# Plain tiles in place of two Strassen quads for one head group, another order of one group's band sets, and later queue clocks in the plan

## The chip, the cores and the metric

The kernel runs on one core of a Trainium2 chip. The metric is the time on the device in microseconds (us). The kernel before takes 650.26 us, the median of 3 runs from 650.11 to 650.94. Its profile shows one execution, with a span of 648.3 us from the first to the last instruction.

## The reference

Two branches work on the same `x` of 2048 tokens by 1024 and are mixed by a gate. Branch A is attention with 32 heads of 32 channels, in which each token looks at 8 tokens at a distance of 2. Branch B is a gated MLP with a product along the sequence.

```python
def _A_ref(x, wqkv, wo):
    H, Dh, W, dil = 32, 32, 8, 2
    q, k, v = ...                                  # x @ wqkv, by heads
    idx = pos[:, None] - (jnp.arange(W) * dil)[None, :]
    logits = einsum('bhsd,bhswd->bhsw', q, k[idx]) * Dh ** -0.5   # masked where idx < 0
    attn = softmax(logits)
    return einsum('bhsw,bhswd->bhsd', attn, v[idx]) @ wo

def _B_ref(x, w_in, w_sp, b_sp, w_out):
    z = gelu(x @ w_in)
    z1, z2 = z[..., :Fh], layernorm(z[..., Fh:])   # Fh = 1792
    g = einsum('ts,bsf->btf', w_sp, z2) + b_sp
    return (z1 * g) @ w_out

g = sigmoid((x * gate_w).sum(-1, keepdims=True))
out = g * A + (1 - g) * B
```

## The kernel before

The heads are worked on in 8 groups of 4 heads (128 channels). For each group TensorE makes q and k, transposed, then the band: for every block of 64 tokens the products with the 71 keys that it can see. ScalarE copies the band out of PSUM, it goes to DRAM and comes back in a skewed layout (`att_L`), and VectorE does the softmax and the products with v. All this is interleaved with the large products of both branches on TensorE. A plan made at build time, with a clock for each engine and for the transfer queue (`SP`, `DMA`), decides where in each engine's order the attention operations and transfers are put.

There are two ways to make q and k of a group. The plain way has 8 tiles of 8 matmuls, each 512 columns:

```python
def qk_tile(g, t, c, bank=low_bank):               # t: q or k, c: 512 tokens
    ps = bank()
    for kt in range(KT):                           # KT = 8
        nc.tensor.matmul(ps[:], w[:, t, kt, :], xT[:, kt, 512 * c:512 * (c + 1)], ...)
    act(0.5, pe(T_QK) + 0.2)
    nc.scalar.copy(dst[:, :, 256 * c:256 * (c + 1)], ps[:]...)
```

The Strassen way (Winograd's form) has two quads. A quad makes two blocks of q and two of k with 7 products of 4 matmuls in place of 8 products; it needs sums of the weights (`qk_sums`) and of `x` (`x_sums`, in `xts`), and copies and adds between the PSUM banks:

```python
def chain(...):                                    # used by qk_quad and z2_quad; generator
    X, Y, Z, V = bank_roles[side]                  # four banks: 0 to 3 or 4 to 7
    product(X, pairs(A11, B11), True, N);  nc.scalar.copy(Y[:, n], X[:, n]);  yield    # seed
    product(V, pairs(S1, T1), True, N);    share(vs, V[:, n]);                yield
    product(Y, pairs(S2, T2), False, N);   plus(Z, Y);                        yield    # VectorE add
    product(X, pairs(A12, B21), False, N); put(0, 0, X);                      yield
    product(Y, pairs(S3, T3), False, N);   plus(V, Y); put(1, 1, V);          yield
    product(Z, pairs(S4, B22), False, N);  put(0, 1, Z);                      yield
    product(W, pairs(A22, T4), False, N);  put(1, 0, W);                      yield
```

Two small matmuls (`mark`) go ahead of a quad on banks in which its later products are to add to what another engine wrote. Groups 2 to 5 are Strassen quads in both kernels. In the kernel before group 1 is too: its quads run one after the other, alone, and start just before the gate's transpose:

```python
    def x_sums(c): ...                             # 4 sums of 2048 elements for half c
    for c in range(4):                             # start: q, k of group 0, v of groups 0 to 2, bands of group 0
        ...
        if c > 1:
            x_sums(c - 2)
        if c == 2:
            load_wqk(2, sync.dma_start)
        ...
    for f in qk_sums(1):
        f()
    first_quad = qk_quad(1, 0, 0)
    for _ in range(2):
        next(first_quad)
    gate_mm = nc.tensor.matmul(glT, gl_s[:], ident32[:], start=True, stop=True)
    ...                                            # tanh, two VectorE operations, two stores
    settle(); live[0] = True                       # from here the plan is in force
    band_data[0], band_free[0], v_data[0] = T_START        # (0.0, 0.0, 0.0)
    clock["SP"], clock["DMA"] = 0.5, 1.5
    next_bands(); ...                              # att_L of group 0, g_att, v of group 0
    dma(0.0, 3.7, load_wvr, lambda t: fill.extend(... sums4_steps(wvs, ...)))   # weights of v_quad and their sums
    load_wqk_later(3, 0.0)

    def play_group(g):
        if g == 0:
            run(first_quad, step=step)
            run(qk_quad(1, 1, 0), step=step)
        elif g + 1 in PAIRS: ...                   # PAIRS = (2, 4)
```

The v of groups 0 to 2 is stored to DRAM by GpSimd's queue while the kernel starts:

```python
            (nc.gpsimd if i < 16 else sync).dma_start(dv, st[:, :, g * C:(g + 1) * C])
```

The band of a group is made in three sets, 0 with 2 blocks (16 matmuls) and 1 and 2 with 7 (56 matmuls). All use banks 4 to 7, so ScalarE must have copied one set out before the next is made. Group 7 has no next group to prepare; its sets stand among four plain tiles of z2 (8 matmuls of 448 columns each), after which the quads of z2 follow in pairs, one on each side:

```python
    BAND_SETS = [(0, 8, 2), (1, 1, 7), (9, 1, 7)]
    def group_tiles(g):                            # last line: g = 7
        ...
        return [tiles[0], band[1], tiles[1], band[0], tiles[2], band[2], tiles[3]]
    ...
        def quad_step():
            if n == 0 and count[0] == 0:
                mark(bank_roles[1][1:3], ZC)
            step(); ...
        run(*[z2_quad(*q) for q in quads[n:n + 2]], step=quad_step)
```

Of the kernel before, what the change touches and what calls it, by code (L numbers as in the profile page):

```python
# [13 lines left out]
P = 128  # L14
S = 2048
D = 1024
# [4 lines left out]
NG = NH // HG  # L21
# [37 lines left out]
def kernel(  # L59
# [238 lines left out]
    def vp_tile(i, bank=None, middle=None):  # L298
        ps = bank() if bank else banks[i % 2]
        for kt in range(KT):  # L300
            if kt == (2 if i else 6) and middle is not None:
                middle()
            nc.tensor.matmul(ps[:, 0:VP + 1], xT[:, kt, i * P:(i + 1) * P], wvp[:, kt, :], start=(kt == 0), stop=(kt == KT - 1))  # L303
        st = vp_slots[i // 4]
        nc.scalar.copy(st[:, i % 4, :].rearrange("p (g d h) -> p g d h", g=GP, h=HG), ps[:, 0:VP].rearrange("p (g h d) -> p g d h", g=GP, h=HG))
        nc.scalar.copy(gl_s[:, i:i + 1], ps[:, VP:VP + 1])
        if i % 4 == 3:
            for g in range(GP):
                dv = bass.AP(tensor=v_d.tensor, offset=v_d.offset + (g * (S + 16) + 16 + (i - 3) * P) * C, ap=[[C, P], [P * C, 4], [1, C]])
                (nc.gpsimd if i < 16 else sync).dma_start(dv, st[:, :, g * C:(g + 1) * C])  # L310

# [68 lines left out]
    def first_bands(c):  # L380
        band_blocks(0, *((0, 8, 2), (1, 1, 6, 3), (4, 1, 4, 2), (6, 1, 4, 2))[c])

    def x_sums(c):
        for r in range(4):
            lo, hi = slice(512 * c, 512 * c + 512), slice(1024 + 512 * c, 1536 + 512 * c)
            a, b = ((xT[:, 0:4, hi], xT[:, 0:4, lo]), (xT[:, 4:8, hi], xts[0][:, :, lo]),
                    (xT[:, 4:8, hi], xT[:, 0:4, hi]), (xT[:, 4:8, lo], xts[1][:, :, lo]))[r]
            nc.vector.tensor_tensor(xts[r][:, :, lo], a, b, ALU.subtract)  # L388

    quad = [0]  # L390
# [75 lines left out]
    def chain(A11, A12, A22, S1, S2, S3, S4, B11, B21, B22, T1, T2, T3, T4, vs, put, share, N, flip=False, side=None, lean=False, done=None):  # L466
# [8 lines left out]

        if side is None:
            side = quad[0] % 2
            quad[0] += 1
        X, Y, Z, V = bank_roles[side]
        bank_roles[side] = [X, V, Y, Z] if lean else [Y, V, X, Z]  # L480
        n = slice(0, N)
        dur, copy = N / 600.0 + 0.01, N / 1400.0 + 0.22
# [345 lines left out]
    LEAN = (True, True)  # L828
    T_START = (0.0, 0.0, 0.0)

    def square(n, x, junk):
# [6 lines left out]
        return nc.scalar.activation(junk, src, ACT.Square, accum_out=(s2, s2h)[x][:, n:n + 1])  # L838

    NQ = (0, 0, 0, 0, 0, 0, 0, 0)  # L840
    quads = [(0, i) for i in range(7)] + [(1, i) for i in range(8)]
# [3 lines left out]
    qv_slots = [reg(R_OFF + 34752 + 1024 * r, 1024).bitcast(F32) for r in range(2)]  # L845
    q_landed, q_free = {}, [1, 1]

# [47 lines left out]
    def play_group(g):  # L895
        if g == 0:
            run(first_quad, step=step)
            run(qk_quad(1, 1, 0), step=step)
        elif g + 1 in PAIRS:
            among_bands(g, qk_quad(g + 1, 0, 0))  # L900
            first = qk_quad(g + 1, 1, 0)
            for _ in range(2):
                next(first)
                step()
            mark(bank_roles[1][1:3], 512)
            run(qk_quad(g + 2, 0, 1), first, step=step)
        elif g in PAIRS:
            among_bands(g, qk_quad(g + 1, 1, 0))
        else:
            return False  # L910
        return True

    def group_tiles(g):
        if g + 1 < NG:
            tiles = [lambda t=t, c=c: qk_tile(g + 1, t, c) for t in range(2) for c in range(4)]
        else:
            tiles = [lambda a=a, m=m: z2_tile(7, a, m) for m in range(2) for a in range(2)]
        if g == 0:
            return tiles

        def band(x):
            band_set(g, x)
            if x == 2:
                bands_have[0] = g + 1
        band = [lambda x=x, f=band: f(x) for x in range(3)]
        if g - 1 in PAIRS and g + 1 < NG:
            return tiles[0:2] + [tiles[2], band[0], tiles[3], band[1], tiles[4], tiles[5], band[2]] + tiles[6:]
        if g + 1 < NG:
            return [tiles[0], band[0], tiles[1], band[1], tiles[2], tiles[3], band[2]] + tiles[4:]
        return [tiles[0], band[1], tiles[1], band[0], tiles[2], band[2], tiles[3]]  # L930

# [37 lines left out]

    for c in range(4):  # L970
        tiles = range(4 * c, 4 * c + 4) if c else ()
        for n, i in enumerate(tiles if c < 3 else ()):
            vp_tile(i, low_bank)
            if n == 0:
                first_bands(c - 1)
        if c > 1:
            x_sums(c - 2)
        if c == 2:
            load_wqk(2, sync.dma_start)
        for t in range(2):  # L980
            qk_tile(0, t, c, (lambda: banks[1 + t]) if c == 3 else low_bank)
            if c == 3 and t == 0:
                first_bands(2)
    for i in tiles:
        vp_tile(i, lambda: banks[3 * (i % 2)])
        if i == 12:
            first_bands(3)
    for f in qk_sums(1):
        f()

    first_quad = qk_quad(1, 0, 0)
    for _ in range(2):
        next(first_quad)
    glT = banks[7][0:16, 0:P]
    gate_mm = nc.tensor.matmul(glT, gl_s[:], ident32[:], start=True, stop=True)
    gate_act = nc.scalar.activation(omg[:], glT, ACT.Tanh, scale=0.5)
    nc.vector.tensor_scalar(g_s[:], omg[:], 0.5, 0.5, ALU.mult, ALU.add)
    gate_vec = nc.vector.tensor_scalar(omg_h[:], omg[:], -0.5, 0.5, ALU.mult, ALU.add)
    sync.dma_start(bass.AP(tensor=g_d.tensor, offset=g_d.offset, ap=[[P, 16], [1, P]]), g_s[:])
    gate_dma = sync.dma_start(bass.AP(tensor=og_d.tensor, offset=og_d.offset, ap=[[P, 16], [1, P]]), omg_h[:])  # L1000

    settle()
# [5 lines left out]
    band_data[0], band_free[0], v_data[0] = T_START  # L1008
    clock["SP"], clock["DMA"] = 0.5, 1.5
    stored.clear()  # L1010
# [3 lines left out]
    next_v(1)  # L1014
    def load_wvr():
        for m in range(2):
            sync.dma_start(wvr[m], wq_v[:, :, 2 * D + VP + VH * m:2 * D + VP + VH * (m + 1)])

    dma(0.0, 3.7, load_wvr, lambda t: fill.extend((t + LATE, 0.75, f) for f in sums4_steps(wvs, wvr[0][:, 0:4], wvr[0][:, 4:8], wvr[1][:, 0:4], wvr[1][:, 4:8])))
    load_wqk_later(3, 0.0)  # L1020
    next_v()
    q_free[:] = [1, 1]
    if 2 in PAIRS:
# [27 lines left out]
    for n in range(0, len(quads), 2):  # L1051
# [10 lines left out]
        def quad_step():  # L1062
            hold[0] = count[0] != 1
            if n == 0 and count[0] == 0:
                mark(bank_roles[1][1:3], ZC)
            step()
            count[0] += 1
            if p == 1 and i < 7 and count[0] in SQ_AT and squares[0][0] < 2 * i and len(squares) > 32 - SQH:
                act(0.9, clock["PE"])
                square(*squares.pop(0), None)  # L1070
        run(*[z2_quad(*q) for q in quads[n:n + 2]], step=quad_step)
    hold[0] = False
# [587 lines left out]
```

## Time and profile before

| what | value |
|---|---|
| time, median of 3 runs | 650.26 us |
| span in the profile | 648.3 us |
| TensorE matmuls | 637.5 us busy, 4345 recorded |
| VectorE | 519.3 us busy |
| ScalarE | 298.1 us busy |
| granted TensorE clock | 1.000 |
| groups 1 to 7 with their bands | about 42 to 181 us |
| z2, z1 and the rest of attention | about 182 to 345 us |

In the rows of slices each digit is the busy tenth of 1/40 of the span, here 16.2 us. In the timelines a row is a run of instructions of one kind: start, duration from the first to the last, engine, line of the kernel, operation, output and input, and their number; in square brackets is the idle time ahead of it and what ended it. PE is TensorE, DVE is VectorE, ACT is ScalarE, and SPq is the queue in which SyncE issues transfers. A few per cent of the matmul records are missing, so a count may be one or two short of the code's.

### The profile page before, as it was taken

Reading aid. Unit: us, or ns where it says so; the run is one execution under the profiler, and the core shown is the slowest. Engines: PE = TensorE matmul, PEld = TensorE weight load, DVE = VectorE, ACT = ScalarE, POOL = GpSimd, SP = SyncE. Lnnn points to the kernel's source line nnn. Section 1 sums busy time; section 2 is a strip of 40 time slices with the busy share of each in tenths; the row PEclk is TensorE's granted clock in tenths of the full one; section 3 lists DMA queues with packets and bytes.
Section 4 is the critical chain, followed back from the end, with each engine's and each line's share of the span. In section 5 each row is a group of like instructions: output and inputs, shape, how many; then the busy total and the mean of one; then the engine's idle time right before and its main releaser. Section 6 shows DMA issues by size and latency. Waiting matters only on the chain.

```text
span 648.3 us, 11298 instructions
## 1 busy us (share of the span) xinstructions
PE 637.5 (98%) x4345; PEld 336.2 (52%) x4391; DVE 519.3 (80%) x816; ACT 298.1 (46%) x644; POOL 15.4 (2%) x27
## 2 busy tenths in 40 slices
PE   8999999999999999999999999999999999999997
PEld 4544467444455555444444444444444444868684
DVE  0347998999899999999988766987569999586852
ACT  3547677676786878799643121121121121202120
POOL 2210000000000000001000000000000000000000
PEclk9999999999999999999999999999999999999999
DMA  9979564798687012258994578369487383557501
GB/s 218 202 162 283 115 153 103 175 226 197 133 216 201 1 51 76 66 160 233 259 257 130 130 166 189 100 202 283 91 190 174 84 158 102 107 138 127 124 28 49
DMA packets 227174, 98.19 MB, mean 151 GB/s; under 512 B 174496, under 2 KB 214064, under 8 KB 227120
## 3 DMA queue, kind: packets, MB, share of 16 engines
q1 hardware_dynamic: 226256, 95.70, 61.2%
q0 software_dynamic: 576, 1.57, 0.9%
q8 instruction: 34, 0.56, 0.4%
q10 hardware_dynamic: 288, 0.20, 0.1%
q14 instruction: 20, 0.16, 0.1%
HBM read 44.31 MB, written 36.61 MB: 125 GB/s over the span
## 4 chain that ended last, share of the span: by engine, by line
PE 90%; ACT 4%; SPq 2%; DMA 1%; DVE 1%; issue 1%; DVEq 0%; ACTq 0%
PE psum_all L402 71%; PE psum_all L1484 8%; PE psum_all L293 6%; PE psum_all L303 2%; PE psum_all L355 2%; ACT arena L838 2%; ACT arena L1175 1%; PE psum_all L790 1%; SPq L178 1%; DMA arena<-in_A_wqkv_dram 1%; SPq L194 1%; ACT arena L363 1%; ACT arena L783 1%; DMA arena<-zg_d 1%; DVE psum_all L473 0%
## 5 line engine op out<-in xcount | busy, mean ns | idle before, releaser
L402 PE MATMUL psum_all<-arena 128*128 128x512 f16 (+6 forms) x2481 | 502.5, 362 | 3.3 <-issue 0.8
L402 PEld LDWEIGHTS <-arena 128*128 128x128 f16 (+1 forms) x2518 | 244.9, 98 | 253.4 <-issue 3.2
L676 DVE TENSOR_TENSOR arena<-arena,att_A 128x2048 f16<-128x2048 bf16 x64 | 75.5, 1220 | 0.3
L473 DVE TENSOR_TENSOR psum_all<-psum_all,arena 128x512 f32<-128x512 f32 (+1 forms) x78 | 51.0, 669 | 8.7 <-PE psum_all L402 5.7
L1484 PE MATMUL psum_all<-arena 128*128 128x256 f16 (+1 forms) x468 | 51.6, 273 | 0.0
L1484 PEld LDWEIGHTS <-arena 128*128 128x128 f16 x468 | 45.8, 98 | 5.5
L293 PE MATMUL psum_all<-arena 128*128 128x512 bf16 x183 | 42.0, 379 | 1.2 <-issue 0.8
L420 ACT COPY psum_all<-psum_all 128x512 f32<-128x512 f32 (+1 forms) x24 | 12.5, 519 | 66.2 <-PE psum_all L402 65.5
L783 ACT ACTIVATE arena<-psum_all 128x448 bf16<-128x448 f32 x64 | 34.2, 545 | 18.3 <-PE psum_all L402 9.0
L1175 ACT ACTIVATE arena<-psum_all 128x512 bf16<-128x512 f32 x56 | 31.4, 613 | 19.8 <-PE psum_all L402 9.0
L680 DVE TENSOR_TENSOR arena<-arena 128x2048 f16<-128x2048 f16 x32 | 37.9, 1218 | 0.0
L363 ACT CAST arena<-psum_all 128x1988 f16<-128x1988 f32 (+3 forms) x25 | 33.9, 1358 | 2.7 <-PE psum_all L355 2.3
L838 ACT ACTIVATE arena<-arena 128x896 bf16<-128x896 bf16 x32 | 30.9, 981 | 0.0
L545 DVE TENSOR_TENSOR arena<-arena 128x512 f16<-128x512 bf16 (+5 forms) x60 | 30.1, 534 | 0.4
L444 ACT COPY psum_all<-psum_all 128x512 f32<-128x512 f32 (+1 forms) x24 | 12.3, 518 | 37.5 <-PE psum_all L402 36.8
L293 PEld LDWEIGHTS <-arena 128*128 128x128 bf16 x192 | 18.1, 98 | 21.5 <-DMA arena<-in_A_wqkv_dram 0.6
L869 ACT CAST arena<-psum_all 128x512 bf16<-128x512 f32 x40 | 22.2, 592 | 12.4 <-DVE psum_all L473 9.8
L388 DVE TENSOR_TENSOR arena<-arena 128x2048 f16<-128x2048 bf16 x8 | 9.4, 1221 | 20.9 <-DMA arena<-in_A_x_dram 20.7
L486 ACT COPY psum_all<-psum_all 128x512 f32<-128x512 f32 (+1 forms) x39 | 21.7, 570 | 6.6 <-PE psum_all L402 6.0
L426 ACT COPY arena<-psum_all 128x512 f32<-128x512 f32 (+1 forms) x24 | 12.7, 533 | 26.1 <-PE psum_all L402 22.5
L431 ACT COPY psum_all<-psum_all 128x512 f32<-128x512 f32 (+1 forms) x24 | 12.4, 517 | 25.8 <-PE psum_all L402 24.8
L549 DVE TENSOR_TENSOR arena<-arena 128x1024 f16<-128x1024 f16 (+1 forms) x16 | 11.4, 715 | 15.7 <-PE psum_all L402 15.7
(113 smaller groups left out, 530.3 us busy)
## 6 DMA issues: line engine op xcount, KB each, us to landing
arena<-v_d SPq DMA_DIRECT2D x8, 960.0 KB, 5.8
z_d<-arena SPq DMA_DIRECT2D x14, 512.0 KB, 3.9
arena<-z_d SPq DMA_DIRECT2D x14, 512.0 KB, 4.4
zg_d<-arena SPq DMA_DIRECT2D x56, 128.0 KB, 2.2
arena<-zg_d SPq DMA_DIRECT2D x32, 224.0 KB, 3.2
band_d<-arena SPq DMA_DIRECT2D x28, 248.5 KB, 4.2
arena<-in_A_wqkv_dram SPq DMA_DIRECT2D x16, 256.0 KB, 4.2
o_d<-arena SPq DMA_DIRECT2D x4, 1024.0 KB, 5.7
```

What stands on the lines that cost most here:

```text
L293: nc.tensor.matmul(ps[:], w[:, t, kt, :], xT[:, kt, 512 * c:512 * (c + 1)], start=(kt == 0), stop=(kt == KT - 1))
L363: nc.scalar.copy(dst, src)
L402: nc.tensor.matmul(bank[:, 0:N], lhsT, rhs, start=(start and m == 0), stop=(m == n - 1), skip_group_check=True)
L473: last_add[0] = nc.vector.tensor_tensor(out[:, n], a[:, n], vs, ALU.add)
L545: return [lambda a=a: nc.vector.tensor_tensor(*a) for a in args]
L676: lambda ws=ws, in0=in0, in1=in1: tt(p5[:, ws], in0[:, ws], in1[:, ws], ALU.mult)), False
L680: lambda a=p3[:, ws], b=p3[:, ws.start + 4:ws.stop + 4]: tt(a, a, b, ALU.add)), not n
L783: nc.scalar.activation(z2[:, i + 8 * a, ZC * c:ZC * (c + 1)], bank[:, 0:ZC], ACT.Gelu_apprx_tanh, accum_out=s1[:, 4 * n + c:4 * n + c + 1])
L838: return nc.scalar.activation(junk, src, ACT.Square, accum_out=(s2, s2h)[x][:, n:n + 1])
L869: nc.scalar.copy((qT_slots, kT_slots)[t][g % 2][:, :, 256 * (c + 2 * x):256 * (c + 2 * x + 1)], bank[:].rearrange("p (n e) -> p e n", e=2))
L1175: last_gelu[0] = nc.scalar.activation(z1s[:, f, a, :], bank[:], ACT.Gelu_apprx_tanh)
L1484: nc.tensor.matmul(bank[:, h], l, r, start=(start and m == 0), stop=(m == len(ab) - 1), skip_group_check=True)
```

## The change

Group 1 is made of plain tiles: one before the gate, seven after it. The sums of `x` are written after the gate. The stores of v go through SyncE's queue, the weights of the v quads are loaded and summed in the start, and the plan's clocks for SyncE and the transfers begin 8 us and 7 us later, so that the plan fits a queue that is still at work on these. In group 7 the small band set moves from between two tiles into the first quad of z2, after that quad's first product; the quad on the other side starts after its second. The rest follows from these: the counter of quads counts all quads, and `q_free` starts with one slot free. The purpose is fewer sums and adds on VectorE around the start of attention, a plan nearer to what the queue does, and no small band set that waits on ScalarE.

```diff
-                (nc.gpsimd if i < 16 else sync).dma_start(dv, st[:, :, g * C:(g + 1) * C])
+                sync.dma_start(dv, st[:, :, g * C:(g + 1) * C])
...
+        if c == 1:
+            for m in range(2):
+                sync.dma_start(wvr[m], wq_v[:, :, 2 * D + VP + VH * m:2 * D + VP + VH * (m + 1)])
...
+    qk_tile(1, 0, 0)
+    (gate, as before)
+    def x_sums(r):
+        for c in range(2): ...
+    for r in range(4):
+        x_sums(r)
...
-    T_START = (0.0, 0.0, 0.0)
+    T_START = (0.5, 0.0, 2.5)
...
+    sums4(wvs, wvr[0][:, 0:4], wvr[0][:, 4:8], wvr[1][:, 0:4], wvr[1][:, 4:8])
...
-        if g == 0:
-            run(first_quad, step=step)
-            run(qk_quad(1, 1, 0), step=step)
-        elif g + 1 in PAIRS:
+        if g + 1 in PAIRS:
...
-            tiles = [lambda t=t, c=c: qk_tile(g + 1, t, c) for t in range(2) for c in range(4)]
+            tiles = [lambda t=t, c=c: qk_tile(g + 1, t, c) for t in range(2) for c in range(4)][not g:]
...
-        return [tiles[0], band[1], tiles[1], band[0], tiles[2], band[2], tiles[3]]
+        return [tiles[0], band[1], tiles[1], tiles[2], band[2], tiles[3]]
...
-    for f in qk_sums(1):
-        f()
-
-    first_quad = qk_quad(1, 0, 0)
-    for _ in range(2):
-        next(first_quad)
...
-    clock["SP"], clock["DMA"] = 0.5, 1.5
+    clock["SP"], clock["DMA"] = 8.5, 8.5
...
-    def load_wvr(): ...
-    dma(0.0, 3.7, load_wvr, lambda t: fill.extend((t + LATE, 0.75, f) for f in sums4_steps(wvs, ...)))
     load_wqk_later(3, 0.0)
...
-            if n == 0 and count[0] == 0:
-                mark(bank_roles[1][1:3], ZC)
...
-        run(*[z2_quad(*q) for q in quads[n:n + 2]], step=quad_step)
+        two = [z2_quad(*q) for q in quads[n:n + 2]]
+        if n == 0:
+            for m in range(2):
+                next(two[0])
+                step()
+                if m == 0:
+                    band_set(NG - 1, 0)
+                    bands_have[0] = NG
+                    step()
+            mark(bank_roles[1][1:3], ZC)
+            two = two[::-1]
+        run(*two, step=quad_step)
```

## The prediction

> **What bounds the kernel now.** I read the page's busy shares first, then the slices, then the chain that ended last, and only then the stretch in which the change acts.
>
> ```profile
> span 648.3 us, 11298 instructions
> ...
> PE 637.5 (98%) x4345; PEld 336.2 (52%) x4391; DVE 519.3 (80%) x816; ACT 298.1 (46%) x644; POOL 15.4 (2%) x27
> ...
> PE   8999999999999999999999999999999999999997
> ...
> DVE  0347998999899999999988766987569999586852
> ...
> PEclk9999999999999999999999999999999999999999
> ...
> PE 90%; ACT 4%; SPq 2%; DMA 1%; DVE 1%; issue 1%; DVEq 0%; ACTq 0%
> ```
>
> TensorE is busy in every slice, at full granted clock, and carries 90% of the chain. VectorE is nearly full from about 55 to 300 us, but it does not hold TensorE up: the list of TensorE's waits over the whole run adds to some 5 us, with no entry after VectorE but two at the start. So time changes by what is added to or taken from TensorE's queue, and by small waits. These are the places the change touches (columns: start, duration, engine, line, operation, count):
>
> ```profile
> 42.63 1.89 PE L402 MATMUL psum_all<-arena 128*128 128x512 bf16 x7
> 44.45 0.39 PE L995 MATMUL psum_all<-ident,gl_s 128*16 128x128 f32 x2
> 44.78 11.83 PE L402 MATMUL psum_all<-arena 128*128 128x512 f16 x51
> 56.53 0.27 PE L355 MATMUL psum_all<-arena 32*64 32x64 bf16 x16
> ...
> 143.17 5.34 PE L293 MATMUL psum_all<-arena 128*128 128x512 bf16 x23
> 148.44 0.27 PE L355 MATMUL psum_all<-arena 32*64 32x64 bf16 x16
> ...
> 175.75 0.65 PE L355 MATMUL psum_all<-arena 32*64 32x71 bf16 x56
> 176.34 1.69 PE L790 MATMUL psum_all<-arena 128*128 128x448 bf16 x8
> 178.64 0.27 PE L355 MATMUL psum_all<-arena 32*64 32x64 bf16 x16 [0.61 <-ACT arena L363]
> ```
>
> Three plain q/k tiles, 24 matmuls (one record is missing), take 148.44 − 143.17 = 5.27 us; about 0.1 us of it is the change-over to the band matmuls. That gives 0.2155 us a matmul, without stalls. The Strassen run from 44.78 to 56.53 is 52 matmuls by the code: 20 left of the first quad, 28 of the second, 4 of the next group's. It takes 11.75 us where 52 × 0.2155 = 11.21, so 0.54 us is lost, 0.1 of it at the change-over. The lost 0.44 us is what a quad that runs alone pays for its adds and copies. The last lines show one real wait: in group 7 the small band set stands 0.61 us because ScalarE still empties the set before it.
>
> The queue that issues the transfers, and the first work that waits for them:
>
> ```profile
> 34.78 8.40 SPq L189 DMA_DIRECT2D band_d<-arena  x12
> 45.90 0.35 SPq L189 DMA_DIRECT2D g_d<-g_s  x1
> 46.35 0.37 SPq L189 DMA_DIRECT2D og_d<-omg_h  x1
> 46.82 1.29 SPq L189 DMA_DIRECT2D att_L<-band_d  x2
> ...
> 49.38 6.63 SPq L189 DMA_DIRECT2D arena<-in_A_wqkv_dram  x4
> ...
> 50.62 0.29 DVE L639 TENSOR_TENSOR att_m<-att_L 128x256 f16<-128x256 f16 x1 [1.93 <-DMA att_L<-band_d]
> ...
> 59.35 1.67 DVE L545 TENSOR_TENSOR arena<-arena 128x1280 f16<-128x1280 bf16 x2
> ```
>
> SyncE's queue is free when the gate is ready at 45.9, so attention starts on VectorE at 50.62, 3.8 us after its load is issued. The sums of the v weights (128x1280) come later, among the attention.
>
> **What the Trainium skill says.** *TensorE: Matmul & The Clock Gate*, section "Wait — 56ns, not 53.3ns?", gives a warm 512-column matmul as 215.7 ns from start to start. The 0.2155 above agrees. *Trainium Kernel Development and Optimization*, section "Key Constraints", says that transfers issued from SyncE, ScalarE and GpSimd share the same 16 DMA engines, and that another queue saves only issue time. The trace has the issue times: 8.40 / 12 = 0.70 us for a band store on SyncE. So moving stores from GpSimd to SyncE costs SyncE's time and no bandwidth. *PSUM — Partial Sum Buffer*, section "PSUM bank collisions raise a hardware error", says two engines must not be in one bank and partition at once. This is why the band matmuls wait for ScalarE in the 0.61 us above. *ScalarE: Activation LUTs*, section "What ACT_TABLE_LOAD costs", has about 1283 ns for a load of a table and 1380 more of drain. The trace shows 1.28 us at 174.95 and the next instruction at 176.25, so no drain here. This load delays the copy of group 7's first band set.
>
> **The change part by part.**
>
> (1) q and k of group 1. Removed: two Strassen quads, 14 products of 4 = 56 matmuls. Added: 8 tiles of 8 = 64. On TensorE's path that is 8 × 0.2155 = +1.72 us. Going from one plain tile to the next cost nothing in the 24-matmul run above, so the 0.44 us of stalls goes away. The gate's transpose stays. Net **+1.28 us**. Beside the path, VectorE loses 4 adds of 0.70 us = 2.8 us and 4 sums (about 1.5 us, done before the gate in idle time); ScalarE has 8 copies of 0.58 in place of 12 operations of that size. Neither bounds this stretch.
>
> (2) v stores on SyncE, v weights loaded early, later queue clocks. SyncE gets 12 stores more and two loads ahead of the attention's loads. At 0.70 us a store this is 8.4 us; the two loads at 6.63 / 4 = 1.66 us are 3.3 us. Its queue was ready at 34.78 + 8.40 = 43.2, so it is now free at about 54.9 at worst. That is 8 to 9 us after the gate's stores were issued, and the plan's new start of 8.5 for the queue says the same. Attention then starts at about 58 in place of 50.6. Against this, VectorE no longer has the adds (2.8 us) nor the v sums (four of about 0.83 = 3.3 us) among its attention work: 6.1 us less. VectorE is thus about 1 us later with its attention, and TensorE is 1.3 us later too. I count **0** for the path. The x sums are written later in the code but wait only for the transposes, so they should still run in VectorE's idle time before the gate.
>
> (3) Group 7. The order becomes tile, large set, two tiles, large set, tile, first product of the z2 quad, small set, second product. The large sets are now two tiles apart, 2 × 1.5 = 3.0 us against the 2.3 us between 176.34 and the end of ScalarE's work on the set, so the 0.61 us goes. But the small set is copied out on ScalarE (0.20 + 0.58 us) behind the quad's first seed copy (0.52 us), and both must be done before the marks on the second side's banks. From the end of the small set to the marks TensorE has only one product, 4 × 448 columns = 0.76 us. Seed and copies end about 1.35 us after the first product, and the small set and second product are done after some 0.2 + 0.1 + 0.76 = 1.05 us plus a change-over. I expect a new wait of 0.3 to 0.6 us there. Net **−0.1 us**.
>
> Sum: 650.26 + 1.28 − 0.1 = 651.4 us.
>
> **The rivals.**
>
> A. *The late attention reaches the path.* If the queue costs more than VectorE's savings, attention ends later than its 292 us, moments and normalization follow late, and TensorE waits where the spatial product begins. For it: VectorE is full, and it ends its spatial weight sums at 345.8, just when they are used. Against it: between 302 and 330 it waits for TensorE eleven times, 2.7 us in all, which it can give. This would make +2 to +4, so 652.5 to 654.
>
> B. *The lighter and better timed VectorE removes waits.* Before, TensorE stands 0.4 us for a copy (L869) at 84.9 and shorter times at 81, 258 to 262 and 290, about 1.9 us in all by the gaps between matmul starts. If the new plan fits the chip better, most go, and the time is 649.3 to 650. For it: the clocks now describe what the queue does. Against it: these waits are on ScalarE, whose order is that of the plan, and moving the plan can as well make others.
>
> C. *Group 1's second Strassen stage waits for a late load.* The weights of group 3 now land about 62 us in place of some 59; four sums must follow before their quad at 66.7. It is some 2 us of slack, so at most about 1 us: 652.4.
>
> **Range and chances.** The counted matmuls are certain; stalls around them move by about 1 us either way. A and C make a tail upward, B a tail downward. I say 651.4 us, 8 times in 10 between 650.0 and 653.2. Either bound of 2% is 13 us away and no part has such a size: faster 0.005, same 0.985, slower 0.01.
>
> **What would show it.** Step 1 is right if group 1 shows 56 to 64 matmuls of the tile's line without stalls, and the first band set of group 1 starts about 57.8 in place of 56.53. Step 2 is right if the attention's first load is issued near 54 and the attention ends within about 2 us of 293. Step 3 is right if the wait at the small set is gone and one of less than 0.6 us stands before the marks. The prediction is wrong if the start of group 1's bands moves by under 0.5 us, or if TensorE shows new waits of over 1 us between 80 and 345 us.

## The result, and the profile after

The changed kernel takes 653.97 us (median of 4 runs, 653.58 to 654.59) where the kernel before takes 650.60 us (650.11 to 651.21): a ratio of 1.0052, 95% interval 1.0035 to 1.0070. It is 3.4 us slower. The prediction was 651.4 us with a range of 650.0 to 653.2, so the time lies above the range. The profiles are of single executions: 650.11 us for the kernel before, the fastest of its runs, and 653.78 us for the changed kernel.

The page of the changed kernel, same parts as before:

```profile
span 652.0 us, 11280 instructions
...
PE 639.7 (98%) x4353; PEld 337.4 (52%) x4399; DVE 515.7 (79%) x808; ACT 295.5 (45%) x640; POOL 6.7 (1%) x15
...
PE 86%; DVE 5%; ACT 4%; DMA 2%; issue 1%; SPq 1%; DVEq 0%
```

TensorE is 2.2 us longer busy, but the span grows by 3.7 us. VectorE did less work than before and still its share of the chain that ended last went from 1% to 5%: TensorE now waits for it. The timeline of TensorE shows where (line numbers are those of the new file: L293 is a plain tile, L434 a Strassen product, L821 a plain z2 tile, L589 a mark):

```profile
44.89 12.26 PE L293 MATMUL psum_all<-arena 128*128 128x512 bf16 x55
56.99 1.03 PE L434 MATMUL psum_all<-arena 128*128 128x512 bf16 x4
57.95 0.27 PE L355 MATMUL psum_all<-arena 32*64 32x64 bf16 x16
...
183.93 0.27 PE L355 MATMUL psum_all<-arena 32*64 32x64 bf16 x16
...
185.50 0.54 PE L589 MATMUL psum_all<-arena 128*128 128x448 bf16 x2 [0.43 <-ACT arena L363]
...
190.28 4.70 PE L434 MATMUL psum_all<-arena 128*128 128x448 f16 x24 [0.46 <-DVE psum_all L505]
195.49 4.70 PE L434 MATMUL psum_all<-arena 128*128 128x448 bf16 x24 [0.50 <-DVE psum_all L505]
...
298.51 5.55 PE L434 MATMUL psum_all<-arena 128*128 128x512 f16 x25 [0.91 <-DVE psum_all L505]
```

Group 1's first band set starts at 57.95 in place of 56.53; the start of the kernel alone is 0.1 us longer in this execution. The wait for ScalarE at group 7's small set is gone, and one of 0.43 us before the marks is there. New are three waits for an add of a Strassen quad on VectorE: 0.46 and 0.50 us in the first quads of z2, and 0.91 us in z1. A fourth, 0.35 us at 263.58, stands where the kernel before waits 0.27 us for ScalarE. VectorE's timeline around these (L707 is a product of attention with v, L711, L712 and L716 sum the products, L505 is the add of a quad, L1172 the copy with which the next pair of z1 quads begins):

```profile
186.20 3.49 DVE L707 TENSOR_TENSOR arena<-arena,att_A 128x2048 f16<-128x2048 bf16 x3
189.60 0.62 DVE L505 TENSOR_TENSOR psum_all<-psum_all,arena 128x448 f32<-128x448 f32 x1
190.14 1.22 DVE L707 TENSOR_TENSOR arena<-arena,att_A 128x2048 f16<-128x2048 bf16 x1
191.27 0.62 DVE L505 TENSOR_TENSOR psum_all<-psum_all,arena 128x448 f32<-128x448 f32 x1
...
192.54 2.35 DVE L711 TENSOR_TENSOR arena<-arena 128x2048 f16<-128x2048 f16 x2
194.80 0.63 DVE L505 TENSOR_TENSOR psum_all<-psum_all,arena 128x448 f32<-128x448 f32 x1
...
286.58 1.29 DVE L505 TENSOR_TENSOR psum_all<-psum_all,arena 128x512 f32<-128x512 f32 x2
287.78 4.62 DVE L707 TENSOR_TENSOR arena<-arena,att_A 128x2048 f16<-128x2048 bf16 x4
292.32 2.35 DVE L711 TENSOR_TENSOR arena<-arena 128x2048 f16<-128x2048 f16 x2
294.70 1.22 DVE L712 TENSOR_TENSOR arena<-arena 128x2048 f16<-128x2048 f16 x1
295.96 0.69 DVE L716 TENSOR_TENSOR arena<-arena 128x1024 f16<-128x1024 f16 x1
296.57 1.28 DVE L1172 COPY arena<-psum_all 128x512 f32<-128x512 f32 x2
297.77 1.29 DVE L505 TENSOR_TENSOR psum_all<-psum_all,arena 128x512 f32<-128x512 f32 x2
```

In each case VectorE does attention work without a pause and the add that TensorE needs stands behind it. The last stretch is the drain: after the second pair of z1 quads the program puts out in one piece whatever is left of attention. Here that is four products and their sums. In the kernel before (L473 is the add there, L676 the product, as L505 and L707 here) it is three, and TensorE does not wait:

```profile
283.82 1.29 DVE L473 TENSOR_TENSOR psum_all<-psum_all,arena 128x512 f32<-128x512 f32 x2
285.02 3.49 DVE L676 TENSOR_TENSOR arena<-arena,att_A 128x2048 f16<-128x2048 bf16 x3
```

The start of attention, from the queue's timeline and VectorE's:

```profile
53.54 1.28 SPq L189 DMA_DIRECT2D att_L<-band_d  x2
```

```profile
57.29 0.29 DVE L670 TENSOR_TENSOR att_m<-att_L 128x256 f16<-128x256 f16 x1 [7.44 <-DMA att_L<-band_d]
```

It begins 6.7 us later than before, and VectorE stands idle for 7.44 us ahead of it. Two theories follow from this: the attention starts too late on the chip (rival A of the prediction), or the order in which the plan writes VectorE's program is at fault, whatever the chip does.

### The profile page after: what moved, and what is told of

It reads as the page before. It is cut to its first block, busy times and chain, and to the rows that moved or that the text cites. A ratio compares the mean times of both kernels' runs of the same rounds, so it can differ in the third digit from the quotient of the medians.

```text
span 652.0 us, 11280 instructions
## 1 busy us (share of the span) xinstructions
PE 639.7 (98%) x4353; PEld 337.4 (52%) x4399; DVE 515.7 (79%) x808; ACT 295.5 (45%) x640; POOL 6.7 (1%) x15
## 4 chain that ended last, share of the span: by engine, by line
PE 86%; DVE 5%; ACT 4%; DMA 2%; issue 1%; SPq 1%; DVEq 0%
PE psum_all L434 67%; PE psum_all L1485 8%; PE psum_all L293 7%; PE psum_all L303 2%; ACT arena L869 2%; DVE arena L707 2%; PE psum_all L355 1%; ACT arena L1176 1%; DVE arena L711 1%; DVE psum_all L505 1%; SPq L178 1%; DMA arena<-in_B_w_in_dram 1%; DMA arena<-in_A_wqkv_dram 1%; DMA band_d<-arena 1%; ACT arena L363 1%
## 5 line engine op out<-in xcount | busy, mean ns | idle before, releaser
L434 PE MATMUL psum_all<-arena 128*128 128x512 f16 (+6 forms) x2427 | 490.5, 361 | 5.5 <-DVE psum_all L505 2.2
L434 PEld LDWEIGHTS <-arena 128*128 128x128 f16 (+1 forms) x2462 | 239.5, 98 | 249.0 <-issue 5.1
L707 DVE TENSOR_TENSOR arena<-arena,att_A 128x2048 f16<-128x2048 bf16 x64 | 75.8, 1219 | 0.3
L293 PE MATMUL psum_all<-arena 128*128 128x512 bf16 x245 | 56.0, 379 | 1.4 <-issue 0.6
L505 DVE TENSOR_TENSOR psum_all<-psum_all,arena 128x512 f32<-128x512 f32 (+1 forms) x74 | 48.3, 668 | 8.5 <-PE psum_all L434 7.4
L293 PEld LDWEIGHTS <-arena 128*128 128x128 bf16 x256 | 24.3, 98 | 29.0 <-DMA arena<-in_A_wqkv_dram 0.7
L711 DVE TENSOR_TENSOR arena<-arena 128x2048 f16<-128x2048 f16 x32 | 37.9, 1218 | 0.0
L296 ACT CAST arena<-psum_all 128x512 bf16<-128x512 f32 x32 | 18.6, 586 | 26.1 <-PE psum_all L293 26.1
L576 DVE TENSOR_TENSOR arena<-arena 128x512 f16<-128x512 bf16 (+3 forms) x52 | 25.4, 522 | 1.6 <-DMA arena<-in_A_wqkv_dram 1.3
L580 DVE TENSOR_TENSOR arena<-arena 128x1024 f16<-128x1024 f16 (+2 forms) x17 | 12.2, 720 | 14.6 <-PE psum_all L434 14.6
```

The lines of the kernel that those rows point to most:

```text
L434: nc.tensor.matmul(bank[:, 0:N], lhsT, rhs, start=(start and m == 0), stop=(m == n - 1), skip_group_check=True)
L505: last_add[0] = nc.vector.tensor_tensor(out[:, n], a[:, n], vs, ALU.add)
L576: return [lambda a=a: nc.vector.tensor_tensor(*a) for a in args]
L707: lambda ws=ws, in0=in0, in1=in1: tt(p5[:, ws], in0[:, ws], in1[:, ws], ALU.mult)), False
L711: lambda a=p3[:, ws], b=p3[:, ws.start + 4:ws.stop + 4]: tt(a, a, b, ALU.add)), not n
```

## The experiments

Each ratio is to the kernel before, timed on the same chip at the same time, with its 95% interval. Single executions of one program differ (the kernel before took 651.0 to 658.2 us beside the last runs), so the ratios are of medians, and a wait read from a profile is that of one execution. Of the rivals to "late on the chip", one is the order of the z2 quads and the other the plan's clocks.

**Stores back on GpSimd, nothing else.** This leaves the order on TensorE, VectorE and ScalarE exactly that of the changed kernel.

```diff
-                sync.dma_start(dv, st[:, :, g * C:(g + 1) * C])
+                nc.gpsimd.dma_start(dv, st[:, :, g * C:(g + 1) * C])
```

> The changed kernel, but the 12 stores of v go through GpSimd's queue again. The order of every instruction on VectorE, ScalarE and TensorE stays that of the changed kernel; only SyncE's queue loses 12 stores of about 0.6 us. Late attention (theory): the first attention operation moves from 57.3 to 50 to 52 us, the three waits of TensorE for VectorE's adds (190.3, 195.5, 298.5; 0.46, 0.50, 0.91 us) shrink to under 0.5 us together, and the time falls from 654.0 to 651.7 to 652.3. Order of the quads (rival): the two waits near 190 and 195 stay, 653 or more. Plan (rival): the order on VectorE is the cause whatever the start, so all three stay and the time is 653.5 or more.

Measured: 1.0038 (1.0026 to 1.0049). Attention starts at 54.95, 2.3 us sooner, and no more, since the early loads of the v weights still stand ahead of it. TensorE's waits do not shrink:

```profile
190.37 4.70 PE L434 MATMUL psum_all<-arena 128*128 128x448 f16 x24 [0.70 <-DVE psum_all L505]
195.58 4.70 PE L434 MATMUL psum_all<-arena 128*128 128x448 bf16 x24 [0.50 <-DVE psum_all L505]
...
298.60 5.55 PE L434 MATMUL psum_all<-arena 128*128 128x512 f16 x25 [0.91 <-DVE psum_all L505]
```

The last is the same to the hundredth. The ratio lies inside the changed kernel's interval, so a start 2.3 us sooner buys nothing that these times show. The reason stands further on in VectorE's timeline: ahead of group 5's softmax it is idle until that group's band has landed, and then goes on at 172.82 here, against 172.72 in the changed kernel. Whatever was won at the start is gone by then. So the theory of a late start of attention falls in its simple form (the start is still 4.3 us later than in the kernel before). The order stays as a suspect.

**Group 7 and the first z2 quads in the order of before**, in the changed kernel:

```diff
-        return [tiles[0], band[1], tiles[1], tiles[2], band[2], tiles[3]]
+        return [tiles[0], band[1], tiles[1], band[0], tiles[2], band[2], tiles[3]]
-        (two steps of the first quad, small set between them, marks, quads swapped)
+        run(*[z2_quad(*q) for q in quads[n:n + 2]], step=quad_step)    # mark after one step, as before
```

> The changed kernel with group 7 and the first z2 quads in the order of the kernel before. Order of the quads (rival): the waits near 190 and 195 go, the 0.61 us before the small set comes back, 652.9 to 653.3. Late attention (theory): VectorE is as late as in the changed kernel, so waits of about the same sum turn up at the next quads, 653.7 to 654.4.

Measured: 1.0017 (1.0004 to 1.0030). The waits near 190 and 195 are gone and do not turn up elsewhere; the wait at the small set is back (0.62 us); the one in z1 stays at 0.91. The wait in z1 is thus not the quads' order. For the two in z2 the profile alone does not decide: group 5's band landed at 171.90 in this execution, 0.8 us sooner than in the changed kernel's, and the first add of z2 ends at 190.53, about when TensorE needs it. With the band as late as there, some 0.7 us of wait would stand here too. (An estimate: with plain tiles alone, below, TensorE waits after 28 matmuls, 5.46 us, behind the marks; here these end at 185.24 + 5.46 = 190.70.) The times do speak for the order: 1.0017 here against 1.0038 in the run above, which has the new order and was timed beside it; the intervals barely overlap.

**The kernel before with its stores on SyncE:**

```diff
-                (nc.gpsimd if i < 16 else sync).dma_start(dv, st[:, :, g * C:(g + 1) * C])
+                sync.dma_start(dv, st[:, :, g * C:(g + 1) * C])
```

> The kernel before, with nothing changed but the 12 stores of v on SyncE's queue. Late attention (theory): attention starts 5 to 7 us later with the plan of before, TensorE gets waits for adds of 1 to 3 us in sum after 180 us, 652 to 653.5. Rivals (order of quads, plan): neither is touched, 650.3 to 651.

Measured: 1.0055 (1.0040 to 1.0070). TensorE waits 2.99 us at 55.64 and 2.08 us at 194.22, both for an add. VectorE's timeline shows the first:

```profile
53.74 0.29 DVE L639 TENSOR_TENSOR att_m<-att_L 128x256 f16<-128x256 f16 x1 [5.30 <-DMA att_L<-band_d]
...
54.90 0.69 DVE L473 TENSOR_TENSOR psum_all<-psum_all,arena 128x512 f32<-128x512 f32 x1
```

The add of group 1's quad stands behind attention operations in VectorE's program, and it runs at 54.90, only after VectorE has stood 5.30 us for their data. The plan expected the data earlier. The second wait has the same form: group 5's band lands only at 174.08 (VectorE stands 3.86 us for it), and the add near 194 is late with it, in the old order of the quads. Late data on the chip do cost, then, through an order made for early data; the cost is larger than expected. This is what the later clocks of the change are for.

**The kernel before with group 1 as plain tiles and nothing else:**

```diff
-    for f in qk_sums(1): f()
-    first_quad = qk_quad(1, 0, 0)
-    for _ in range(2): next(first_quad)
+    qk_tile(1, 0, 0)
-        if g == 0: run(first_quad, step=step); run(qk_quad(1, 1, 0), step=step)
-    q_free[:] = [1, 1]
+    q_free[:] = [1, 0]
```

(and seven tiles in `group_tiles(0)`)

> The kernel before with group 1 as plain tiles and nothing else (stores on GpSimd, clocks and group 7 as before, the v weights loaded and summed where they were). The matmuls alone: TensorE is 1.3 us later at group 1's first band and stays so, 651.7 to 652.2. Late attention (theory): attention starts as early as before, so no more than that. If plain tiles themselves brought the new waits: 653 or more.

Measured: 1.0014 (0.9999 to 1.0029). From group 0's first band set to group 1's TensorE takes 57.93 − 16.42 = 41.51 us, against 56.53 − 16.32 = 40.21 before: +1.30. The changed kernel has 57.95 − 16.44 = 41.51. So the plain tiles cost 1.30 us, and they do not bring the waits of the changed kernel: near 190 there is one of 0.32 us, and in z1 none for VectorE at the drain.

**The kernel before with the new order of group 7 and z2 alone** (the second edit, the other way round):

> The kernel before with only group 7 and the first z2 quads in the new order. Order of the quads (theory now): the 0.61 us before the small set goes, a wait of about 0.4 us before the marks and waits for adds of 0.6 us each near 190 and 195 come, 650.9 to 651.7. Plan (rival): the waits for adds come only with the late clocks, so the order gains or loses nothing, 650.0 to 650.6.

Measured: 1.0023 (1.0008 to 1.0039). The 0.61 us is gone, 0.43 before the marks comes, and TensorE waits 1.45 and 0.63 us for adds in z2 and 0.91 in z1. By the ratio the order costs more than it saves under the plan of before too. The sizes of the z2 waits are partly those of this execution, in which group 5's band landed at 173.09 after VectorE had stood 3.71 us for it, where the kernel before went on at 168.56. The order also changes what is left at the drain, from three products to four.

**The kernel before with the later clocks alone:**

```diff
-    T_START = (0.0, 0.0, 0.0)
+    T_START = (0.5, 0.0, 2.5)
-    clock["SP"], clock["DMA"] = 0.5, 1.5
+    clock["SP"], clock["DMA"] = 8.5, 8.5
```

With these clocks some sums of group 3's weights are written behind the matmuls that read them, so part of q and k of that group is computed from other values; the amount of work is the same.

> The kernel before with only the plan's clocks set later (T_START and the queue's 8.5). On the chip the queue is as free as before. Plan (theory): the attention operations stand later in VectorE's order, one product of 1.2 us more is left when the rest is put out at once in z1, and TensorE waits about 0.9 us there for an add (near 295), with some change of the smaller waits: 651 to 652. If only the real start matters: 650.2 to 650.8.

Measured: 1.0120 (1.0098 to 1.0142). The direction was right and the size far too small: at the drain four products and the sums of the half before them are left, and TensorE waits 5.50 us for the add that follows:

```profile
301.79 2.72 PE L402 MATMUL psum_all<-arena 128*128 128x512 f16 x6 [5.50 <-DVE psum_all L473]
```

With the later plan more of attention is left at the drain, which has a fixed place.

**The changed kernel with the clocks of before and the stores on GpSimd** (the edits above together):

> The changed kernel with the stores on GpSimd and the plan's clocks of before; group 7's new order stays. Plan (theory): the 0.9 us wait near 297 goes, those near 190 and 195 stay if they are the order's, so 652.2 to 653.2. Late attention: as the queue is free sooner too, all waits go, 651.6 to 652.

Measured: 1.0091 (1.0072 to 1.0109). This is slower than both expectations. At the drain one product is left, and TensorE waits for no add there, nor in z2. But attention started at 56.27 in a program whose plan has the queue free 8 us sooner than the changed kernel's plan, and TensorE waits 1.08 us at 58.70 for ScalarE and 2.63 us at 65.94 for an add. The new order of the quads does not bring waits in z2 in every case: after these delays TensorE starts z2 at 181.76, 6.7 us after VectorE goes on with group 5's band (175.02), where the changed kernel has 2.9 us (175.66 and 172.72).

**The drain one round later**, in the changed kernel:

```diff
-    DRAIN, SUMS = 1, NFH - 2
+    DRAIN, SUMS = 2, NFH - 2
```

> The changed kernel with the rest of attention put out one round of z1 later (after the third pair of z1 quads in place of the second), so that it is spread by the plan and not put out in one piece. If what is left at that point is the cause of the 0.91 us wait near 298, the wait goes or shrinks below 0.3 us; the normalization starts later, which may cost some of it again: 653 to 653.9. If it is the late start on the chip, the wait stays: 654 or more.

Measured: 1.0160 (1.0136 to 1.0185), and it does not answer the question. In that round the first spatial weights are loaded into the space of attention's products, which are now still to come; VectorE waits 6.70 us for these loads, and the kernel computes the rest of attention from overwritten data. It shows that the drain cannot stand later: attention has a deadline there.

**One product less at the drain**, in the changed kernel (the last of group 7's last half is left out):

```diff
-   lambda ws=ws, in0=in0, in1=in1: tt(p5[:, ws], in0[:, ws], in1[:, ws], ALU.mult)
+   lambda ws=ws, in0=in0, in1=in1, skip=(g, e, ws.start) == (NG - 1, 1, 6): None if skip else tt(...)
```

> The changed kernel without one instruction: the last of the four products of the last half of group 7's attention is left out (so part of that half's output lacks its new values). Every other instruction and its order stay. Left-over at the drain (theory): TensorE's wait of 0.91 us near 298 (gap 1.07 us) goes, since three products and what follows end in time as in the kernel before; all else stays, so 1.0 to 1.1 us less than the changed kernel. If the wait there has another cause (the start of attention on the chip, ScalarE), it stays or moves by well under 0.5 us.

Measured: 1.0013 (1.0003 to 1.0023). TensorE no longer waits there; its timeline is one unbroken run, and VectorE's drain has three products:

```profile
285.72 18.62 PE L434 MATMUL psum_all<-arena 128*128 128x512 f16 x84
```

```profile
288.19 3.49 DVE L707 TENSOR_TENSOR arena<-arena,att_A 128x2048 f16<-128x2048 bf16 x3
```

The waits in z2 are there as before (0.8 us the longest). So the fourth product, 1.2 us of work that in the kernel before was done ahead of the adds, makes the wait of 0.91 us. The gain in time was not measured side by side: against the ratios of 1.0038 to 1.0052 of the kernels with all four products it is 1.6 to 2.5 us, more than the 1.0 to 1.1 expected.

**The changed kernel with the clocks at 5.0:**

```diff
-    clock["SP"], clock["DMA"] = 8.5, 8.5
+    clock["SP"], clock["DMA"] = 5.0, 5.0
```

> The changed kernel with the plan's two queue clocks at 5.0 in place of 8.5, which leaves one product at the drain in place of four; on the chip the queue is as late as in the changed kernel. Plan (theory): no wait near 298; the adds near 190 and 195 stand in another order, so those waits change too; if the attention's first data are late against this plan, TensorE waits 1 us or more for an add near 60 to 64. In sum 652.5 to 654. If the plan is not the cause: 653.5 to 654.5 with the wait near 298 as before.

Measured: 1.0026 (1.0016 to 1.0037). One product is left at the drain, and the wait in z1 is gone with the queue as late as ever (attention starts at 57.47). In exchange TensorE waits where attention is late against the plan:

```profile
60.39 1.02 PE L434 MATMUL psum_all<-arena 128*128 128x512 f16 x4 [1.25 <-ACT psum_all L517]
```

It was expected to wait for an add. It waits for a copy of ScalarE, which stands behind attention's exponential, and that waits 2.74 us for VectorE's first attention operations. In z2 waits of 0.21 and 0.37 us for adds remain. The clocks trade one wait for another.

**The changed kernel again**, beside the next two:

> The changed kernel, unchanged, on the same chip as the next two, so that these are compared with it. TensorE's waits as in its first profile: gaps between matmul starts of about 0.6 and 0.7 us near 190 and 195 and 1.07 us near 298; 1.003 to 1.006 of the kernel before.

Measured: 1.0040 (1.0022 to 1.0057). Attention starts at 58.67 in this execution, the wait near 190 is 1.60 us, the next 0.50 and the drain's 0.91. What sets the first can be read from VectorE's timelines. This is the first operation on group 5's band in the kernel before, in the changed kernel's first profile and in this one:

```profile
168.56 0.29 DVE L639 TENSOR_TENSOR att_m<-att_L 128x256 f16<-128x256 f16 x1 [2.17 <-DMA att_L<-band_d]
```

```profile
172.72 0.29 DVE L670 TENSOR_TENSOR att_m<-att_L 128x256 f16<-128x256 f16 x1 [1.90 <-DMA att_L<-band_d]
```

```profile
175.01 0.29 DVE L670 TENSOR_TENSOR att_m<-att_L 128x256 f16<-128x256 f16 x1 [2.22 <-DMA att_L<-band_d]
```

From here to the first add of z2 VectorE works without a pause, for 16.88 us in the changed kernel (to 189.60) and 16.87 us in this execution (to 191.88). So the add comes later by what the band comes later. In the kernel before this work takes longer, 19.47 us, but the band was there 5.6 us ahead of TensorE's first z2 tile (174.15), against 2.9 us in the changed kernel. In the five executions with the changed kernel's order up to there, the wait near 190 is 0.46, 0.70, 0.76, 0.83 and 1.60 us, with the band 2.9, 2.7, 2.6, 2.5 and 0.7 us ahead. It thus depends on when data land and on what the order puts between. The drain's wait does not: it is 0.91 us in all six profiles that leave just four products there.

**One product less ahead of the add in z2** (the third of group 4's first half; the edit of the drain with another number):

> The changed kernel without one instruction: the third of the four products of group 4's first half, which stands in VectorE's order ahead of the add for which TensorE waits near 190 (that half then lacks its new values). Left-over ahead of the add (theory): the gap near 190 goes, and that near 195 goes or shrinks, as VectorE is 1.2 us sooner there; the gap near 298 stays at 1.07, since the drain's order is the same. If the wait near 190 has another cause (ScalarE's table loads, the marks, the banks of the second side), it stays.

Measured: 1.0017 (0.9995 to 1.0040). Both waits in z2 are gone; TensorE runs on from the marks:

```profile
185.90 13.33 PE L434 MATMUL psum_all<-arena 128*128 128x448 bf16 x69
```

and the drain's wait is 0.91 us still. Group 5's band landed at 172.72, as in the changed kernel's first profile, so the missing product alone makes this difference. The waits in z2 come from what stands ahead of the adds, not from the marks or the banks.

**The order of before and one product less at the drain**, in the changed kernel, to see whether anything is left over:

> The changed kernel with group 7 and the first z2 quads in the order of before and without the last product at the drain: both kinds of new wait are taken away. What is left over the kernel before should be the 8 matmuls less the quads' stalls, 1.3 us, and the larger wait near 86 (0.2 us): 1.5 us, a ratio of 1.001 to 1.003, and in the profile no new gap of over 0.3 us after 180 but the old 0.6 us before the small set. If the ledger misses a cost, more than that remains.

Measured: 0.9998 (0.9974 to 1.0023). The interval holds the 1.5 us expected and also nothing, so it does not close the sum. Its profile cannot either: in that execution the data of another group land late (VectorE stands 3.88 us for them before 176.65), ScalarE's exponential waits with them, and TensorE then waits 1.9 us for ScalarE's band copies, 1.8 us for its tile copies and 1.12 us for an add at 195.35, with the quads in the order of before. The wait in z1 is gone in it.

**A version from what was learned**: the kernel before with Strassen quads for group 1, early clocks and the quads of z2 unswapped, and the small set moved ahead of group 7's first tile, where ScalarE has long copied the last large set out. As the program is then written, that move alone would leave four products at the drain; with the plan's overhang `FR` at 0.35 it leaves two.

```diff
-        return [tiles[0], band[1], tiles[1], band[0], tiles[2], band[2], tiles[3]]
+        return [band[0], tiles[0], band[1], tiles[1], tiles[2], band[2], tiles[3]]
-    FR, LATE, WZ_LATE = 0.4, 0.5, 4.0
+    FR, LATE, WZ_LATE = 0.35, 0.5, 4.0
```

> The kernel before with group 7's small set ahead of its first tile in place of between the second and third, and with the plan's overhang FR at 0.35 in place of 0.4 (so that two products are left at the drain and the adds of z2 stay in pairs). The 0.61 us wait for ScalarE before the small set goes and nothing replaces it: 0.4 to 0.7 us under the kernel before. If the small set waits for the copies of the last tiles instead: no gain.

Measured: 0.9983 (0.9973 to 0.9994), so 1.1 us under the kernel before (0.4 to 1.8 by the interval), and under both kernels. No wait stands in group 7:

```profile
175.19 0.27 PE L355 MATMUL psum_all<-arena 32*64 32x64 bf16 x16
175.39 1.69 PE L790 MATMUL psum_all<-arena 128*128 128x448 bf16 x8
177.01 0.65 PE L355 MATMUL psum_all<-arena 32*64 32x71 bf16 x56
```

In this execution other waits stand in its place: 0.75 us for an add at 53.82, where attention started at 51.92, and 0.86 us at 190.28, where group 5's band landed at 171.26. That nothing replaces the 0.61 us is thus not shown by the profile; only the median speaks for it.

**FR at 0.35 alone**, as the control:

> The kernel before with FR at 0.35 alone, which leaves one product at the drain in place of three. As three already cost TensorE nothing, 650.0 to 650.8 or within 0.3 us of the kernel before; the 0.61 us wait in group 7 stays.

Measured: 1.0005 (0.9992 to 1.0018). One product is left at the drain, and this gains nothing over three. Its profile is that of its slowest execution, with a wait of 2.12 us for an add at 191.47. The gain of the version above thus goes with the place of the small set; the two intervals just touch, so its size is uncertain.

## Why the prediction was wrong, point by point

**Step 1 was right.** +1.28 us was predicted and +1.30 measured, in the changed kernel and in the one with plain tiles alone.

**Step 2 is where it failed**: "I count 0 for the path". The inputs were good: attention was to start at about 58 and started at 57.29; the load was to be issued near 54 and was at 53.54. The term that was wrong is "VectorE is thus about 1 us later with its attention". The last sum of group 0's first half starts at 78.23 in place of 72.85, 5.4 us later. The 6.1 us of work taken away did not make up for the late start: two of the four adds had stood ahead of attention (45.87 and 47.66), and from its first operation to its last sum that half takes 21.63 us in place of 22.92, only 1.3 us less. Nor could less work help for long, since VectorE stands idle for group 5's band in both kernels (2.17 and 1.90 us). What counts there is when the band lands. Its load is issued at 167.19 in place of 163.54, and VectorE goes on 4.2 us later with TensorE only 1.5 us later. The prediction's own sign was that attention ends within about 2 us of 293; it ends at 296.65 (295.96 and 0.69).

The more serious gap was in the reasoning: I asked how late attention would be on the chip and not how the plan would write it. VectorE's order is fixed when the program is built. In the changed kernel the clocks at 8.5 leave four products at the drain and those at 5.0 leave one, and the drain stands as one block ahead of the next adds. The fourth product is 0.91 us of wait; taking it away takes the wait away. The number left is not a simple function of the clocks: the new order alone raised it from three to four in the kernel before, and with the clocks of before the changed kernel left one.

**Step 3 was right in its own terms and left something out.** The 0.61 us went, and 0.43 us came before the marks where 0.3 to 0.6 was expected: net −0.2 for the −0.1 predicted. Not foreseen was that the swapped quads spread the adds. In the kernel before they come in pairs, with attention in the long gaps between:

```profile
183.17 4.62 DVE L676 TENSOR_TENSOR arena<-arena,att_A 128x2048 f16<-128x2048 bf16 x4
...
188.03 1.16 DVE L473 TENSOR_TENSOR psum_all<-psum_all,arena 128x448 f32<-128x448 f32 x2
...
191.37 1.16 DVE L473 TENSOR_TENSOR psum_all<-psum_all,arena 128x448 f32<-128x448 f32 x2
```

In the changed kernel they come singly. Its two waits are 0.46 + 0.50 us. How much of this comes from the order (this step) and how much from the late band of group 5 (step 2) was not separated: each run that changes the order also has another landing.

The sum in the changed kernel's profile: 1.30 for the matmuls, −0.61 + 0.43 in group 7, 0.96 in z2, 0.91 at the drain, 0.68 in place of 0.44 us for the wait near 86 and 0.35 in place of 0.27 near 260 make 3.3 us of the 3.7 between the spans; 0.1 is the start, and each new wait has a short change-over that its idle time does not count.

**The rivals.** A named the right engine and about the right size (+2 to +4), and attention does end later; but the place was wrong, since the spatial product never waits, and a sooner start alone brings nothing that could be measured. (VectorE's eleven waits between 302 and 330 sum to 3.0 us, not 2.7.) B did not happen: none of the waits near 81 to 86 and 258 to 265 went away without another of at least the same size in its place, and the one near 86 grew. C did not happen: no wait for a sum or a load stands near 66.7.

The prediction puts the 0.61 us before the small set down to two engines in one PSUM bank. That a set may not be overwritten before ScalarE has copied it would hold TensorE just as long, and no run separates the two.

What stays open: why the wait near 86 grew by 0.24 us with plain tiles alone (0.7 us there too) was not tried; why group 5's load is issued later was not tried either; and the sum was not closed by a run with all new waits taken away.

## What to carry to other kernels

When an engine runs in order and its program is written by a plan, ask of a change two things: when the data come on the chip, and what now stands ahead of the instruction that the bounding engine waits for. Work put out in one piece at a deadline cost nothing here up to three products, and 0.91 us with a fourth of 1.2 us. Work saved on an engine that later stands idle for data, as VectorE does for group 5's band, is lost again there. Moving the small set to a place where its buffer had long been free beat hiding it among the quads.

## What the runs showed of the hardware that I had not expected

The landing of the first attention data varies between executions: the first operation comes at 57.29, 58.17, 57.58 and 58.67 us in kernels with the same order of the queue up to there. The first and the last are the same program; from the issue of the load to the operation it took 3.75 us (from 53.54) in one and 5.24 us (from 53.43) in the other. An order that fits only the early case turns such a delay into a wait of TensorE. The kernel with the new order of group 7 alone has the program of the kernel before up to that point; in its profiled execution attention started at 52.79 in place of 50.62, and TensorE waited 1.43 us at 54.68, which the kernel before did not in its own. In the version with the small set first it started at 51.92, and TensorE waited 0.75 us at 53.82.
